# k and v of two batches laid out as nine tokens a partition, q transposed as it is loaded, and wider rows for the weights

## The chip, the cores and the metric

One Trainium2 chip, of which the kernel uses one core. Its engines run side by side, each through a list of instructions of its own: TensorE (PE, with its weight loads PEld), VectorE (DVE), ScalarE (ACT), GpSimd (POOL) and SyncE (SP), which here issues nearly all DMAs. The metric is the device time of one execution in microseconds (us), compared by the median of several runs.

## The reference

```python
kv = np.einsum('bhsd,bhse->bhde', k, v)          # q, k, v: 4 batches, 8 heads, 576 tokens, 64 wide
out = np.einsum('bhsd,bhde->bhse', q, kv)
rms = np.sqrt(np.mean(out * out, axis=-1, keepdims=True) + 1e-06)
x = out / rms * g_norm                           # then heads side by side: 2304 x 512
h = (x @ w1) * (x @ w2) @ w3                     # 512 -> 1024 -> 1024, float64 weights
x = h @ w_out                                    # 1024 -> 512
p = domain_probs / (domain_probs.sum(-1, keepdims=True) + 1e-09)
for e in range(4):
    out += p[:, e:e + 1] * (np.maximum(x @ e_w1[e], 0.0) @ e_w2[e])   # 512 -> 1024 -> 512
```

## The kernel before

The work goes through three parts. **Attention**: a `unit b p` takes two heads of batch b. It loads q, k and v of 512 of the 576 tokens as 128 partitions of four tokens each, forms k-transposed times v of both heads on PE (`outer`, L717; a fifth step takes the 64 tokens that are left, from tiles `kvr` that `rest_kv` loads for all heads of a batch), copies the two 64x64 results into a block-diagonal tile `kvb`, reorders q by token (`qs`, L733/L734), transposes it on PE (`turned`, L688), multiplies (`inner`, L745), and normalises (`normed_turned`: squares with sums on ACT, L596; a power on POOL, L609; a product on DVE, L612; a transpose; the scale by `g8`). A `rest_unit` does the 64 left tokens of two batches (L780). **The bilinear part**: products of x with w1 and w2 (`bilinear_plain`, `bilinear_pair`), their product element by element, and a product with w3 times w_out, which `row` forms beforehand. **The experts**: for each of three groups of tokens and four experts an `up` and a `down` product, in a form with seven instead of eight block products; the weights' sums and splits are made once, written to DRAM (`w2kept`, `we`) and read again for the later groups.

Large products are done as three passes of fp32r operands split in a high and a low part (`mm3`, L327 to L329; L1574 in the wide down products). The small ones of the attention are plain f32; an f32 product counts as two records on PE in the trace.

What order the instructions stand in is not written by hand. Each function adds operations with the engines that may do them, an assumed cost, and the tiles that they read and write; `Plan.order` lists them by simulated time, with priority by stage, the place in the list `FRONT` (and behind it the loops of the experts). Every engine then runs its list in that order. While PE has nothing to do at the start, two kinds of dummy products fill its list: ten of the tile `warm` (L424), and two or three (L1822) ahead of the first use of each PSUM bank that an operation of stages 1 to 3 takes:

```python
            for b in spare:
                for _ in range(FILL.get(op.prio, 0)):
                    nc.tensor.matmul(b[:, 0:P], ident, ident, start=True, stop=True)
            op.emit(e)
```

They stand in PE's list like any other, and run also when data is there. The vector g is loaded as 128 single elements on ACT's queue (L428).

Of the kernel before, what the change touches and what calls it, by code (L numbers as in the profile page):

```python
# [18 lines left out]
P = 128  # L19
RAWS = 5  # L20
# [11 lines left out]
SUMMING = 18  # L32
# [67 lines left out]
class Plan:  # L100
# [11 lines left out]
    def add(self, engines, emit, reads=(), writes=(), latency=0.2, stage=None, free=False, hold=None):  # L112
# [4 lines left out]

        op = Op(engines, emit, self.stage if stage is None else stage, latency)
# [24 lines left out]
    def order(self):  # L143
# [43 lines left out]
        while len(result) < len(ops):  # L187
# [9 lines left out]
            for e in engines:  # L197
# [26 lines left out]
                end = now + op.engines[e]  # L224
# [5 lines left out]
                op.done = end + op.latency  # L230
# [32 lines left out]
def attention_moe_kernel(  # L263
# [48 lines left out]
    plan = Plan({"r": RAWS, "h": TILES, "n": 4, "c": 2, "b": BANKS, "d": 1000, **RINGS})  # L312
# [5 lines left out]
    def bank():  # L318
        return Buf("b", "b", [P, 512], F32)

# [25 lines left out]
    def load(buf, *parts, key=None, queue="sp", cost=None):  # L346
        def emit(_):
# [6 lines left out]
            {queue: cost or (1.48 if buf.kind == "r" else 0.68)}, emit,  # L354
# [56 lines left out]
    graw = const.tile([P, 1], F32, name="graw")  # L411
# [5 lines left out]
    def constants():  # L417
        make_identity(nc, ident)
        nc.gpsimd.memset(power, -0.5)

        nc.scalar.activation(out=graw, in_=ident[:, 0:1], func=ACTF.Square)
# [27 lines left out]
    def decode(name, src, shape=None):  # L449
# [6 lines left out]
        load(raw, ((lambda t: t.rearrange("p (k f) -> p k f", k=KD)) if shape else whole, src))  # L456
# [110 lines left out]
    def rest_kv(b):  # L567
# [1287 lines left out]
```

## Time and profile before

| | before |
|---|---|
| median of 3 runs | 1107.79 us (1107.46 to 1109.48) |
| the profiled execution: its own time, its span | 1109.42 us, 1107.6 us |
| busy: PE, DVE, ACT, POOL | 99%, 78%, 56%, 4% of the span |
| chain that ended last | PE 94%, DMA 3%, ACT 1%, POOL 1% |
| DMA | 282.30 MB, mean 255 GB/s |
| granted clock of PE | 1.0 in all slices |

The span runs from the first to the last instruction. Busy time is the time in which at least one record of an engine is open; matmuls are pipelined, so that a record of PE stays open beyond the start of the next one. What one more matmul costs is therefore read from the chain or from the starts of successive rows, not from its mean duration.

### The profile page before, as it was taken

How to read it: one execution, taken by the hardware profiler on the slowest of the kernel's cores; microseconds unless marked ns; L12 is line 12 of the kernel's file. 1: busy time of each engine (PE TensorE's matmuls, PEld its weight loads, DVE VectorE, ACT ScalarE, POOL GpSimd, SP SyncE). 2: the span in 40 equal slices, each digit the busy share in tenths (PEclk: the TensorE clock that was granted, in tenths of full speed). 3: DMA queues.
4: the chain of work that ended last, by engine and by line, in shares of the span. 5: the costliest groups of instructions: out<-in, count | busy, mean ns of one | idle time of the engine just before them, and what ended most of it. 6: DMA issues, size and time to landing. Idle time of an engine off the chain costs nothing.

```text
span 1107.6 us, 18599 instructions
## 1 busy us (share of the span) xinstructions
PE 1093.7 (99%) x6376; PEld 993.9 (90%) x6376; DVE 864.2 (78%) x1723; ACT 616.5 (56%) x1500; POOL 47.0 (4%) x57
## 2 busy tenths in 40 slices
PE   7999999999999999999999999999999999999998
PEld 6888888888888999999998999999999999999998
DVE  4888888889869887878888884557788866485896
ACT  6998754656636665754564465443455555444531
POOL 4513200000000000000000000000000000000000
PEclk9999999999999999999999999999999999999999
DMA  9999993441230499988999996878779877686856
GB/s 262 292 345 331 379 359 124 135 155 37 88 103 17 156 334 352 355 304 285 353 356 355 369 348 222 284 237 283 239 240 356 298 222 257 226 290 219 278 154 196
DMA packets 176862, 282.30 MB, mean 255 GB/s; under 512 B 22144, under 2 KB 89728, under 8 KB 176768
## 3 DMA queue, kind: packets, MB, share of 16 engines
q1 hardware_dynamic: 176448, 280.85, 76.1%
q8 instruction: 50, 0.82, 0.3%
q10 hardware_dynamic: 320, 0.26, 0.1%
q14 instruction: 44, 0.36, 0.1%
HBM read 198.22 MB, written 82.84 MB: 254 GB/s over the span
## 4 chain that ended last, share of the span: by engine, by line
PE 94%; DMA 3%; ACT 1%; POOL 1%; DVE 0%; issue 0%; SPq 0%; POOLq 0%; DVEq 0%
PE b L327 24%; PE b L329 24%; PE b L328 24%; PE b L1574 18%; PE b L688 2%; DMA kv<-in_v_dram 1%; PE b L745 1%; PE b L717 1%; DMA w<-w2kept 1%; DMA graw<-in_g_norm_dram 0%; POOL ss L609 0%; DMA we<-wel 0%; DMA woraw<-in_moe_w_out_dram 0%; PE b L780 0%; ACT x L596 0%
## 5 line engine op out<-in xcount | busy, mean ns | idle before, releaser
L676 ACT COPY u<-b 128x384 f32<-128x384 f32 (+1 forms) x191 | 96.4, 505 | 209.3 <-PE b L329 202.3
L1574 PE MATMUL b<-w,hth 128*128 128x512 f32 x588 | 208.2, 394 | 0.3 <-DVE acc L1602 0.2
L1410 DVE TENSOR_TENSOR u<-u,b 128x384 f32<-128x384 f32 x144 | 79.5, 552 | 117.9 <-PE b L329 59.3
L1574 PE MATMUL b<-w,htl 128*128 128x256 f32 x588 | 153.9, 279 | 0.0
L1574 PEld LDWEIGHTS b<-w,hth 128*128 128x128 f32 x588 | 108.4, 188 | 19.0 <-DVE acc L1602 0.9
L1574 PEld LDWEIGHTS b<-w,htl 128*128 128x128 f32 x588 | 110.6, 188 | 3.8
L1602 DVE SCALAR_TENSOR_TENSOR acc<-b,pn,acc 128x512 f32<-128x512 f32 x123 | 85.5, 745 | 29.1 <-PE b L1574 28.4
L372 ACT CAST hth<-s 128x384 fp32r<-128x384 f32 x144 | 70.0, 512 | 48.3 <-DVE s L1510 45.6
L1421 ACT ACTIVATE u<-u 128x384 f32<-128x384 f32 x108 | 56.9, 527 | 44.0 <-DVE u L1410 43.7
L377 DVE TENSOR_TENSOR htl<-s,hth 128x384 fp32r<-128x384 f32 x144 | 75.4, 551 | 3.4 <-ACT hth L372 3.1
L329 PE MATMUL b<-wdh,htl 128*128 128x512 f32 x144 | 56.7, 394 | 0.0
L377 DVE TENSOR_TENSOR htl<-u,hth 128x384 fp32r<-128x384 f32 x108 | 56.0, 551 | 0.8 <-ACT hth L372 0.7
L328 PE MATMUL b<-wdl,hth 128*128 128x512 f32 x144 | 56.6, 393 | 0.0
L327 PE MATMUL b<-wdh,hth 128*128 128x512 f32 x144 | 56.0, 389 | 0.0
L372 ACT CAST hth<-u 128x384 fp32r<-128x384 f32 x107 | 51.5, 510 | 2.4 <-PE b L329 2.0
L327 PE MATMUL b<-w,hth 128*128 128x256 f32 x168 | 47.6, 284 | 1.3 <-DMA w<-w2kept 1.3
L328 PE MATMUL b<-w,hth 128*128 128x256 f32 x168 | 47.5, 283 | 0.0
L329 PE MATMUL b<-w,htl 128*128 128x256 f32 x168 | 47.5, 283 | 0.0
L327 PE MATMUL b<-th,weh 128*128 128x512 f32 x112 | 44.6, 398 | 0.2 <-ACT u L676 0.2
L329 PE MATMUL b<-th,wel 128*128 128x512 f32 x112 | 43.7, 390 | 0.0
L328 PE MATMUL b<-tl,weh 128*128 128x512 f32 x112 | 43.7, 390 | 0.0
L956 DVE TENSOR_TENSOR u<-u,b 128x512 f32<-128x512 f32 x42 | 28.7, 686 | 16.0 <-PE b L329 9.2
(297 smaller groups left out, 3165.5 us busy)
## 6 DMA issues: line engine op xcount, KB each, us to landing
w<-w2kept SPq DMA_DIRECT2D x126, 512.0 KB, 4.4
we<-we SPq DMA_DIRECT2D x240, 256.0 KB, 5.3
we<-weh SPq DMA_DIRECT2D x48, 256.0 KB, 4.4
we<-wel SPq DMA_DIRECT2D x48, 256.0 KB, 4.2
e2raw<-in_moe_w_dram SPq DMA_DIRECT2D x40, 256.0 KB, 4.5
w3raw<-in_moe_w_dram SPq DMA_DIRECT2D x16, 512.0 KB, 3.8
e1raw<-in_moe_w_dram SPq DMA_DIRECT2D x32, 256.0 KB, 4.6
w2kept<-wth SPq DMA_DIRECT2D x32, 256.0 KB, 4.4
```

The costliest lines, as they stand in the source:

```text
L327: nc.tensor.matmul(ps, w[0], x[0], start=first, stop=False, skip_group_check=more)
L328: nc.tensor.matmul(ps, w[0], x[1], start=False, stop=False, skip_group_check=more)
L329: nc.tensor.matmul(ps, w[1], x[0], start=False, stop=last, skip_group_check=more)
L372: nc.scalar.copy(to(dst.high.tile), value(src.tile))
L377: nc.vector.tensor_tensor(out=to(dst.low.tile), in0=value(src.tile), in1=to(dst.high.tile), op=ALU.subtract)
L676: lambda e: nc.scalar.copy(to(dst.tile), value(src.tile)) if e == "act"
L688: nc.tensor.transpose(ps[:, c], raw[:, c], ident)
L956: lambda _: nc.vector.tensor_tensor(out=t.tile, in0=t.tile, in1=ps.tile, op=ALU.add),
L1410: lambda _: nc.vector.tensor_tensor(out=t[:, :W], in0=base[:, :W], in1=ps[:, :W], op=ALU.add),
L1421: lambda eng: nc.scalar.activation(out=t[:, :W], in_=src[:, :W], func=ACTF.Relu)
L1574: nc.tensor.matmul(ps.tile if whole_width else ps[:, 0:256], (h.high if whole_width else h.low)[:, c], both if whole_width else raw[:, r, ...
L1602: nc.vector.scalar_tensor_tensor(out=a.tile, in0=ps.tile, scalar=sc, in1=a.tile, op0=ALU.mult, op1=ALU.add)
```

## The change

Batches 0 and 1 (`NINE`) load k and v of all 576 tokens in one piece a head: 64 partitions a head hold nine consecutive tokens each, so a row of 2,304 bytes is read where it was 1,024. Their product is `outer_by_head` (nine steps for each of two heads, each on 64 partitions and 64 columns), and `kvr` isn't needed for them. In batches 2 and 3 the left tokens come as 32 partitions of two tokens, in two tiles of four heads each, and `outer` has six steps instead of five, whose results for both heads go to PSUM partitions 0 to 63, side by side. q is transposed as it was loaded (`qs` is gone); for that each head's k-v product stands twice on the diagonal of a 128x128 block (`kvb` becomes two tiles), and the reordering by token is done by the access pattern of L612's successor (`by_token`). `rest_unit` multiplies head by head, 64 columns each. w1 and w2 are loaded as 256 rows by 256 columns (rows of 2,048 bytes instead of 1,024), the experts' first weights as 256 columns (1,024 bytes instead of 512), so the blocks f and f+1 now go together instead of f and f+4. g is loaded as a row and turned by a product on PE. `w2kept` is one DRAM buffer for each pair of operands and half, where it was one for each expert, and a read waits only for the writes of its own buffer. Some units' squares are summed on DVE instead of ACT (`EARLY`). The planner has other costs, and `FRONT` is a new list, which begins with the units of batch 1.

```diff
-SUMMING = 18
+NINE = (0, 1)
+TRAFFIC = 1.02
+MARGIN = {"act": 0.1, "dve": 0.1, "sp": 0.2}
+EARLY = (2, 3, 4, 5, 8, 15, 16)
...
 FRONT = (
-    "norm_scale, weight 0 7, unit 1 3, unit 1 2, weight 1 4, weight 1 0, unit 1 0, unit 1 1, unit 0 0, "
...
+    "norm_scale, unit 1 2, unit 1 3, weight 1 4, unit 1 1, weight 1 0, unit 1 0, unit 0 1, unit 0 2, unit "
...
-    graw = const.tile([P, 1], F32, name="graw")
+    graw = const.tile([1, P], F32, name="graw")
...
-            nc.scalar.dma_start(out=graw[i * D:(i + 1) * D], in_=g_norm.rearrange("(d o) -> d o", o=1))
-        nc.vector.tensor_scalar(out=g8, in0=graw, scalar1=float(D) ** 0.5, scalar2=None, op0=ALU.mult)
+            nc.scalar.dma_start(out=graw[:, i * D:(i + 1) * D], in_=g_norm.rearrange("(o d) -> o d", o=1))
...
-        kvr[b] = [half("kvr") for _ in (k, v)]
-        for raw, src in zip(kvr[b], (k, v)):
-            add({"pool": 0.4}, lambda _, raw=raw: nc.gpsimd.memset(raw[REM:P], 0.0), writes=[(raw, 1)])
...
+    kvr_slots = {}
+
+    def rest_kv(b, j):
+
...
+        kvr[b, j] = kvr_slots[turn, j]
+        for raw, src in zip(kvr[b, j], (k, v)):
             load(
-                raw, (lambda t: t[0:REM].rearrange("p (h d) -> p h d", d=D), rest(src, b)),
-                key=0, cost=1.05,
+                raw,
+                (
+                    lambda t: t[0:REM // 2].rearrange("p (h r d) -> p h r d", h=HP, r=2),
+                    src[b, j * HP:(j + 1) * HP, M:S, :].rearrange("h (p r) d -> p h r d", r=2),
+                ),
+                key=0, cost=0.33,
...
-        summing = SUMMING > len(summed)
+        summing = len(summed) not in EARLY
...
         def scale(e):
+            if by_token:
+                nc.vector.tensor_tensor(
+                    out=t.tile.rearrange("p (r h d) -> p h r d", r=R, h=2), in0=heads(ps.tile),
+                    in1=ss.tile.rearrange("p (h r) o -> p h r o", h=2).to_broadcast([P, 2, R, D]), op=ALU.mult,
+                )
+                return
...
     def unit(b, p):
         first = b not in kvb
         if first:
-            kvb[b] = zeroed("kvb")
+            kvb[b] = [zeroed("kvb"), zeroed("kvb")]
         loaded = []
-        for name, src in (("q", q), ("kv", k), ("kv", v)):
+        for name, src in (("q", q), ("kv", k), ("kv", v))[:1 if b in NINE else 3]:
             raw = half(name, ring="attention")
-            load(raw, (heads, head_pair(src, b, p)), cost=0.82)
+            load(raw, (heads, head_pair(src, b, p)), cost=0.8)
             loaded.append(raw)
-        qraw, ks, vs = loaded
-        if first:
-            rest_kv(b)
-        kr, vr = kvr[b]
+        qraw = loaded[0]
+        if b in NINE:
+            kv = Buf("r", "kv", [P, 2, S], F32)
+            load(kv, *(
+                (lambda t, n=n: t[:, n], src[b, 2 * p:2 * p + 2].rearrange("h (g r) d -> (h g) (r d)", g=D))
+                for n, src in enumerate((k, v))
+            ), cost=1.72)
+        else:
+            ks, vs = loaded[1:]
+            if (b, p // 2) not in kvr:
+                rest_kv(b, p // 2)
+            kr, vr = kvr[b, p // 2]
         ps = bank()
 
+        def outer_by_head(e):
+            for r in range(S // D):
+                for h in range(2):
+                    c, m = slice(h * D, (h + 1) * D), slice(r * D, (r + 1) * D)
+                    nc.tensor.matmul(
+                        ps[c, c], kv[c, 0, m], kv[c, 1, m], start=r == 0, stop=r == S // D - 1,
+                        skip_group_check=True,
+                    )
+
         def outer(e):
-            for r in range(R + 1):
+            for r in range(R + 2):
                 for h in range(2):
-                    c = slice(h * D, (h + 1) * D)
                     if r < R:
                         a, b_ = heads(ks.tile)[:, h, r, :], heads(vs.tile)[:, h, r, :]
                     else:
-                        m = slice(p * P + h * D, p * P + (h + 1) * D)
-                        a, b_ = kr[:, m], vr[:, m]
-                    nc.tensor.matmul(ps[c, c], a, b_, start=r == 0, stop=r == R)
-
-        add({"pe": 0.9}, outer, reads=[ks, vs, kr, vr], writes=[ps])
+                        at = (p % 2 * 2 + h) * 2 * D + (r - R) * D
+                        a, b_ = kr[:, at:at + D], vr[:, at:at + D]
+                    nc.tensor.matmul(
+                        ps[0:D, h * D:(h + 1) * D], a, b_, start=r == 0 and h == 0, stop=r == R + 1,
+                        skip_group_check=True,
+                    )
+
+        if b in NINE:
+            add({"pe": 1.4}, outer_by_head, reads=[kv], writes=[ps])
+        else:
+            add({"pe": 0.9}, outer, reads=[ks, vs, kr, vr], writes=[ps])
+        own, at = kvb[b][p // 2], p % 2 * 2 * P
+        parts = []
         for i in range(2):
-            c = slice(i * D, (i + 1) * D)
-            evacuate(
-                kvb[b], ps, D, lambda t, i=i, c=c: t[c, p * P + i * D:p * P + (i + 1) * D],
-                lambda t, c=c: t[c, c], key=(p, i),
-            )
-        qs = half("qs")
-
-        def by_token(t):
-            return t.rearrange("p (r h d) -> p h r d", r=R, h=2)
-
-        add(
-            {"act": t_act(512), "dve": t_fast(512)},
-            lambda e: nc.scalar.copy(by_token(qs.tile), heads(qraw.tile)) if e == "act"
-            else nc.vector.tensor_copy(out=by_token(qs.tile), in_=heads(qraw.tile)),
-            reads=[qraw], writes=[qs],
-        )
-        pq = turned(qs)
+            for h in range(2) if b in NINE else (None,):
+                d = slice(i * D, (i + 1) * D)
+                n, heads_of = (P, slice(0, 2)) if h is None else (D, slice(h, h + 1))
+                rows = slice(0, D) if h is None else slice(h * D, (h + 1) * D)
+                parts.append((own, (p, i, h)))
+                add(
+                    {"act": t_act(n, True), "dve": t_dve(n)},
+                    lambda e, d=d, heads_of=heads_of, rows=rows: (
+                        nc.scalar.copy if e == "act" else nc.vector.tensor_copy
+                    )(
+                        own[d, at:at + 2 * P].rearrange("p (h c) -> p h c", h=2)[:, heads_of, d],
+                        ps[rows, 0:P].rearrange("p (h c) -> p h c", h=2)[:, heads_of],
+                    ),
+                    reads=[ps], writes=parts[-1:], free=True,
+                )
+        pq = turned(qraw)
         qt = half("qt")
         evacuate(qt, pq, 512, whole, whole)
         po = bank()
 
         def inner(e):
-            for r in range(R):
-                c = slice(r * P, (r + 1) * P)
-                nc.tensor.matmul(po[:, c], qt[:, c], kvb[b][:, p * P:(p + 1) * P], start=True, stop=True)
-
-        add({"pe": 0.86}, inner, reads=[qt, (kvb[b], (p, 0)), (kvb[b], (p, 1))], writes=[po])
+            for j in range(4):
+                c, m = slice(j * P, (j + 1) * P), at + j // 2 * P
+                nc.tensor.matmul(po[:, c], qt[:, c], own[:, m:m + P], start=True, stop=True)
+
+        add({"pe": 0.86}, inner, reads=[qt] + parts, writes=[po])
         xr[b, p] = half("xr")
         if b == B - 1 and p < HP // 2:
-            normed_turned(po, [], xr[b, p])
+            normed_turned(po, [], xr[b, p], True)
         else:
             xt[b, p] = Pair("xt")
-            normed_turned(po, [(512, xt[b, p], whole, whole, None)], xr[b, p])
+            normed_turned(po, [(512, xt[b, p], whole, whole, None)], xr[b, p], True)
...
-            for h in range(HP):
-                c = slice(h * P, (h + 1) * P)
+            for h in range(H):
+                c = slice(h // 2 * P, (h // 2 + 1) * P)
                 for i in range(2):
-                    nc.tensor.matmul(po[:, c], qs[i][:, c], kvb[2 * g + i][:, c], start=i == 0, stop=i == 1)
-
-        add({"pe": 1.72}, inner, reads=[qs[0], qs[1], kvb[2 * g], kvb[2 * g + 1]], writes=[po])
+                    own, at = kvb[2 * g + i][h // 4], h % 4 * P + h % 2 * D
+                    nc.tensor.matmul(
+                        po[:, h * D:(h + 1) * D], qs[i][:, c], own[:, at:at + D], start=i == 0, stop=i == 1
+                    )
+
+        add({"pe": 1.72}, inner, reads=qs + kvb[2 * g] + kvb[2 * g + 1], writes=[po])
...
-            weights[n, f] = decode(f"w{n + 1}", columns((moe_w1, moe_w2)[n], f), True)
+            half_, i = divmod(f, KF // 2)
+            src = (moe_w1, moe_w2)[n][half_ * 256:(half_ + 1) * 256, i * 256:(i + 1) * 256]
+            weights[n, f] = decode(f"w{n + 1}", src.rearrange("(k p) f -> p k f", p=P), 2)
...
-        if e not in w2_kept:
-            w2_kept[e] = Buf("d", f"w2kept{e}", [P, len(W2_OPERANDS), KF // 2, 2, 256], F32, tag=f"w2kept{e}")
-        kept, n = w2_kept[e], which[1] - which[0]
+        n = which[1] - which[0]
+        for k in range(*which):
+            if (e, k, i // 2) not in w2_kept:
+                name = f"w2kept{e}_{which[0]}_{i // 2}"
+                w2_kept[e, k, i // 2] = (
+                    w2_kept[e, which[0], i // 2][0] if k > which[0]
+                    else Buf("d", name, [P, n, 2, 2, 256], F32, tag=name), k - which[0],
+                )
+        kept = w2_kept[e, which[0], i // 2][0]
         add(
             {"sp": 0.37 * n},
             lambda _: nc.sync.dma_start(
-                out=kept.tile[:, which[0]:which[1], i, part, :],
+                out=kept.tile[:, :, i % 2, part, :],
                 in_=t.tile.bitcast(F32)[:, 0:256 * n].rearrange("p (o c) -> p o c", o=n),
             ),
-            reads=[t], writes=[(kept, (which, i, part))], latency=2.4,
+            reads=[t], writes=[(kept, (i, part))], latency=2.4,
...
-        raw1, raw2 = Buf("r", "e1raw", [P, 2, 512], F32), Buf("r", "e2raw", [P, 2, 512], F32)
+        raw1, raw2 = Buf("r", "e1raw", [P, KD, 256], F32), Buf("r", "e2raw", [P, 2, 512], F32)
+        load(raw1, (whole, e_w1[e][:, i * 256:(i + 1) * 256].rearrange("(k p) f -> p k f", p=P)))
+        load(raw2, (whole, e_w2[e][i * 256:(i + 1) * 256, :].rearrange("(n p) c -> p n c", p=P)))
         fs = (i, i + KF // 2)
-        load(raw1, *(
-            (lambda t, n=n: t[:, n].rearrange("p (k f) -> p k f", k=KD), columns(e_w1[e], f))
-            for n, f in enumerate(fs)
-        ))
-        load(raw2, *((lambda t, n=n: t[:, n], e_w2[e][f * P:(f + 1) * P, :]) for n, f in enumerate(fs)))
-        w, _ = winograd_weights([raw1, raw1], [lambda t: t[:, 0], lambda t: t[:, 1]])
+        w = expert_operands(raw1)
...
     def norm_scale():
-        add({"act": 1.4}, load_norm, writes=[xscale], latency=2.5, stage=3)
+        row_ = Buf("c", "grow", None, None)
+        row_.tile = graw
+        add({"act": 1.4}, load_norm, writes=[row_], latency=3.5, stage=3)
+        ps = bank()
+        add(
+            {"pe": 0.1}, lambda _: nc.tensor.transpose(ps[:, 0:1], graw, ident[0:1, 0:1]),
+            reads=[row_], writes=[ps],
+        )
+        add(
+            {"dve": 0.2},
+            lambda _: nc.vector.tensor_scalar(
+                out=g8, in0=ps[:, 0:1], scalar1=float(D) ** 0.5, scalar2=None, op0=ALU.mult
+            ),
+            reads=[ps], writes=[xscale], free=True,
```

The experts' weight functions (`expert_operands`, `w2_sums`) form the same sums with fewer and wider DVE instructions; they add nothing to PE's list.

PE's list from its start to the first inner products, before. `warm` and the products of `ident` alone are the dummies, `kv` and `kvr` are the tiles of k and v, `qs` the reordered q:

```order
L424 MATMUL warm<-ident 128x128 x10
L1822 MATMUL b<-ident 128x128 x3
L688 MATMUL b<-ident,qs 128x128 x4
L1822 MATMUL b<-ident 128x128 x3
L717 MATMUL b<-kv 64x64 x8
L717 MATMUL b<-kvr 64x64 x2
L1822 MATMUL b<-ident 128x128 x2
L688 MATMUL b<-ident,qs 128x128 x8
L1822 MATMUL b<-ident 128x128 x3
L745 MATMUL b<-kvb,qt 128x128 x4
```

And the same stretch of the change (L756 is `outer_by_head`, L2027 the dummies, L724 the transposes, L804 `inner`):

```order
L438 MATMUL warm<-ident 128x128 x10
L2027 MATMUL b<-ident 128x128 x3
L724 MATMUL b<-ident,q 128x128 x4
L1950 MATMUL b<-ident,graw 128x1
L2027 MATMUL b<-ident 128x128 x3
L756 MATMUL b<-kv 64x64 x18
L2027 MATMUL b<-ident 128x128 x3
L724 MATMUL b<-ident,q 128x128 x4
L2027 MATMUL b<-ident 128x128 x3
L756 MATMUL b<-kv 64x64 x18
L2027 MATMUL b<-ident 128x128 x3
L804 MATMUL b<-kvb,qt 128x128 x4
```

A unit's outer product is 18 products where it was 10, and there are 24 dummies of L2027 in the whole list where L1822 had 20. In both lists all of these dummies stand ahead of the first large product. Ahead of it stand, before, 52 transposes, 8 units' outer and 7 units' inner products; in the change 56 transposes, 8 outer products of `NINE` and one of batch 3, and 8 inner products. The rows just ahead of the first large product of the change (L341; L769 is `outer` of batches 2 and 3):

```order
L804 MATMUL b<-kvb,qt 128x128 x4
L769 MATMUL b<-kv 64x64 x8
L769 MATMUL b<-kvr 64x64 x4
L724 MATMUL b<-ident,x 128x128 x4
L804 MATMUL b<-kvb,qt 128x128 x8
L724 MATMUL b<-ident,x 128x128 x4
L756 MATMUL b<-kv 64x64 x18
L724 MATMUL b<-ident,q 128x128 x4
L341 MATMUL b<-xth,wh 128x512
```

In batches 2 and 3 a unit's outer product is 12 products (rows L769) where it was 10. All other counts on PE are the same in both lists, the large products' too, except for the one transpose of g (L1950) and for `rest_unit`. There, before, PE had this row in each of the two (`qr` is the turned q of the left tokens):

```order
L780 MATMUL b<-kvb,qr 128x128 x8
```

And in the change:

```order
L840 MATMUL b<-kvb,qr 128x64 x16
```

So as many columns go through, in twice as many products. SP's list at its start, before:

```order
L349 DMA w1raw<-in_moe_w_dram 128x4x128
L349 DMA q<-in_q_dram 128x2x256
L349 DMA kv<-in_k_dram 128x2x256
L349 DMA kv<-in_v_dram 128x2x256
L349 DMA kvr<-in_k_dram 64x8x64
L349 DMA kvr<-in_v_dram 64x8x64
```

And in the change:

```order
L363 DMA q<-in_q_dram 128x2x256
L363 DMA kv<-in_k_dram 128x576
L363 DMA kv<-in_v_dram 128x576
L363 DMA q<-in_q_dram 128x2x256
L363 DMA kv<-in_k_dram 128x576
L363 DMA kv<-in_v_dram 128x576
L363 DMA w2raw<-in_moe_w_dram 128x2x256
```

The first unit's data stands first, and no transfer of `kvr` is among the first 26; the first weights come behind two units.

## Rows read from the trace of the kernel before

**Rows 1.** The page: span, busy time, and slices of 27.7 us.

```profile
span 1107.6 us, 18599 instructions
PE 1093.7 (99%) x6376; PEld 993.9 (90%) x6376; DVE 864.2 (78%) x1723; ACT 616.5 (56%) x1500; POOL 47.0 (4%) x57
...
PE   7999999999999999999999999999999999999998
...
PEclk9999999999999999999999999999999999999999
```

**Rows 2.** Windows: start:end and length, busy time (records) of each engine, clock, DMA.

```profile
core 0: us, PE busy (x) PEld busy (x) DVE busy (x) ACT busy (x) POOL busy (x), PEclk, DMA share, GB/s
0.00:10.00 10.00, 7.10 (x52) 6.80 (x52) 1.61 (x4) 3.80 (x6) 6.71 (x19) 1.00 0.88 213
...
30.00:40.00 10.00, 9.48 (x111) 8.15 (x111) 8.23 (x16) 9.94 (x60) 6.64 (x7) 1.00 1.13 270
40.00:60.00 20.00, 20.00 (x129) 17.02 (x129) 16.91 (x32) 18.58 (x76) 9.19 (x9) 1.00 1.08 313
...
1080.00:1107.60 27.60, 23.10 (x193) 22.89 (x191) 18.00 (x40) 3.88 (x8) 0.00 (x0) 1.00 0.63 196
```

**Rows 3.** The chain that ended last, around 50 and 103 us: start, length, what.

```profile
50.51 0.73 PE b L717 x20
51.24 0.59 PE b L688 x4
...
53.22 0.44 PE b L688 x4
...
55.05 0.89 PE b L745 x8
...
103.70 1.79 PE b L780 x16
```

**Rows 4.** PE's timeline: start, length, records, idle time before and its end.

```profile
1.34 4.64 PE L424 MATMUL warm<-ident 128*128 128x128 f32 x20 [1.34 <-POOL ident masks.py:199]
5.77 0.88 PE L1822 MATMUL b<-ident 128*128 128x128 f32 x6
...
19.86 0.69 PE L717 MATMUL b<-kv 128*64 128x64 f32 x16 [1.70 <-DMA kv<-in_v_dram]
...
36.71 0.48 PE L327 MATMUL b<-xth,wh 128*128 128x512 f32 x1
...
50.44 0.69 PE L717 MATMUL b<-kv 128*64 128x64 f32 x16
50.95 0.29 PE L717 MATMUL b<-kvr 128*64 128x64 f32 x4
51.17 0.66 PE L688 MATMUL b<-ident,qs 128*128 128x128 f32 x4
```

**Rows 5.** Weight loads and products of L717 and L780: durations in ns.

```profile
L717 PEld LDWEIGHTS b<-kv x256: 132/138/138, 9.0 to 111.3; 128*64 128x64 f32 x128
L717 PE MATMUL b<-kv x256: 222/222/271, 9.0 to 111.4; 128*64 128x64 f32 x128
...
L780 PEld LDWEIGHTS b<-kvb,qr x32: 190/192/192, 103.4 to 127.4; 128*128 128x128 f32 x32
L780 PE MATMUL b<-kvb,qr x32: 275/275/275, 103.5 to 127.5; 128*128 128x128 f32 x32
```

**Rows 6.** DMA in the first 45 us: GB/s in 40 slices, totals, issues.

```profile
GB/s 0 44 293 362 309 272 168 173 312 251 260 266 343 369 355 351 342 351 291 168 167 223 283 288 277 301 322 357 350 317 180 181 217 212 295 348 350 348 278 176
DMA packets 15446, 12.09 MB, mean 269 GB/s; under 512 B 4637, under 2 KB 15442, under 8 KB 15442
...
kvr<-in_k_dram SPq DMA_DIRECT2D x4, 128.0 KB, 8.2
```

**Rows 7.** ACT's groups ahead of the first large product: count, busy, mean ns.

```profile
L596 ACT ACTIVATE x<-b 128x64 f32<-128x64 f32 x49 | 10.2, 249 | 1.2 <-PE b L745 1.2
...
L733 ACT COPY qs<-q 128x512 f32<-128x512 f32 x5 | 3.1, 614 | 0.0
```

**Rows 8.** PE's timeline at the one long stop behind the front.

```profile
486.65 0.39 PE L327 MATMUL b<-w,hth 128*128 128x256 f32 x1 [1.32 <-DMA w<-w2kept]
```

More of the change, by code (lines that the diff above doesn't have):

```diff
@@ L110, in __init__, with add @@
         self.stage = 0
-    def add(self, engines, emit, reads=(), writes=(), latency=0.2, stage=None, free=False, hold=None):
+    def add(self, engines, emit, reads=(), writes=(), latency=None, stage=None, free=False, hold=None):
+        if latency is None:
+            latency = 0.2 if "pe" in engines else 0.04
         op = Op(engines, emit, self.stage if stage is None else stage, latency)
@@ L223, in order @@
                     queue[o].remove(op)
-                end = now + op.engines[e]
+                end = now + op.engines[e] * (TRAFFIC if e == "sp" else 1.0)
                 if e in op.ported:
@@ L229, in order @@
                 free_at[e] = end
-                op.done = end + op.latency
+                op.done = end + op.latency + MARGIN.get(e, 0.0)
                 result.append((op, e))
@@ L455, in decode @@
         raw = Buf("r", name + "raw", [P, 512], I64)
-        load(raw, ((lambda t: t.rearrange("p (k f) -> p k f", k=KD)) if shape else whole, src))
+        load(raw, ((lambda t: t.rearrange("p (k f) -> p k f", k=shape)) if shape else whole, src))
         val, add_ = half("val", ring="decoded"), half("add", I32, "decoded")
@@ L618, in normed_turned @@
         if summing:
-            add({"act": 8 * t_act(D, True)}, square, reads=[ps], writes=[t, ss])
+            add({"act": 1.75}, square, reads=[ps], writes=[t, ss])
         else:
@@ L622, in normed_turned @@
             add({"dve": t_dve(512)}, total, reads=[t], writes=[ss], free=True)
-        add({"pool": 1.91}, root, writes=[ss], hold=0.3)
+        add({"pool": 2.2}, root, writes=[ss], hold=0.3)
         add({"dve": t_dve(512)}, scale, reads=[ps, ss], writes=[t], free=True)
@@ L669, in zeroed @@
         t = half(name)
-        add({"pool": 0.5}, lambda _: nc.gpsimd.memset(t.tile, 0.0), writes=[t])
+        cleared(t, (0, P))
         return t
@@ L759, in rest_unit @@
             (lambda t: t[0:REM].rearrange("p (h d) -> p h d", d=D), rest(q, 2 * g)),
-            (lambda t: t[REM:P].rearrange("p (h d) -> p h d", d=D), rest(q, 2 * g + 1)), cost=1.5,
+            (lambda t: t[REM:P].rearrange("p (h d) -> p h d", d=D), rest(q, 2 * g + 1)), cost=2.0,
         )
@@ L998, in bilinear_pair @@
         if g:
-            for j, f in enumerate((f0, f1)):
-                multiplied(B, f, [w[j] for w in ws])
+            for f in (f0, f1):
+                multiplied(B, f, ws)
             return
@@ L1330, in w2_sums @@
             raw = Buf("r", "e2raw", [P, 2, 512], F32)
-            load(raw, *(
-                (lambda t, n=n: t[:, n], e_w2[e][f * P:(f + 1) * P, :]) for n, f in enumerate((i, i + KF // 2))
-            ))
-        def part(n, c):
-            return lambda: [raw[:, n, c * 256:(c + 1) * 256]]
-        def own(t, c):
-            return lambda: [t[:, c * 256:(c + 1) * 256]]
-        t12, t34 = half("t12"), half("t34")
-        lo, hi = slice(0, 256), slice(256, 512)
-        combined("t1", 256, part(0, 1), part(0, 0), ALU.subtract, [raw], t12, lo)
@@ L1344, in w2_sums @@
-        combined("t2", 256, part(1, 1), own(t12, 0), ALU.subtract, [raw, (t12, 0)], t12, hi)
-        combined("t3", 256, part(1, 1), part(0, 1), ALU.subtract, [raw], t34, lo)
-        combined("-t4", 256, part(1, 0), own(t12, 1), ALU.subtract, [raw, (t12, 256)], t34, hi)
-        for t, which in ((t12, (3, 5)), (t34, (5, 7))):
-            s = Pair("wt")
-            split(s, t, 512)
+            load(raw, (whole, e_w2[e][i * 256:(i + 1) * 256, :].rearrange("(n p) c -> p n c", p=P)))
+        t23 = half("t23")
@@ new lines, in sums @@
+        def sums(make, reads, writes, n):
+            add({"dve": t_dve(n)}, make, reads=reads, writes=writes)
+        sums(
+            lambda _: nc.vector.tensor_tensor(
+                out=raw[:, 0, 0:256], in0=raw[:, 0, 256:512], in1=raw[:, 0, 0:256], op=ALU.subtract
+            ), [], [raw], 256,
+        )
+        sums(
+            lambda _: nc.vector.tensor_tensor(
+                out=t23[:, :].rearrange("p (o c) -> p o c", o=2),
+                in0=raw[:, 1, 256:512].unsqueeze(1).to_broadcast([P, 2, 256]),
+                in1=raw[:, 0].rearrange("p (o c) -> p o c", o=2), op=ALU.subtract,
+            ), [raw], [t23], 512,
+        )
@@ new lines, in w2_sums, with two @@
+        sums(
+            lambda _: nc.vector.tensor_tensor(
+                out=raw[:, 1, 0:256], in0=raw[:, 1, 0:256], in1=t23[:, 0:256], op=ALU.subtract
+            ), [t23], [raw], 256,
+        )
+        t14 = Pair("wt")
+        def two(t):
+            return t.rearrange("p (o c) -> p o c", o=2)
+        add(
+            {"act": t_act(512), "dve": t_fast(512)},
+            lambda eng: nc.scalar.copy(two(t14.high.tile), raw[:, :, 0:256]) if eng == "act"
+            else nc.vector.tensor_copy(out=two(t14.high.tile), in_=raw[:, :, 0:256]),
+            reads=[raw], writes=[t14.high],
+        )
@@ L1350, in w2_sums @@
+        add(
+            {"dve": t_dve(512)},
+            lambda _: nc.vector.tensor_tensor(
+                out=two(t14.low.tile), in0=raw[:, :, 0:256], in1=two(t14.high.tile), op=ALU.subtract
+            ),
+            reads=[raw, t14.high], writes=[t14.low],
+        )
+        t23s = Pair("wt")
+        split(t23s, t23, 512)
+        for s, which in ((t14, (5, 7)), (t23s, (3, 5))):
             for n, p in enumerate(s.parts):
@@ L1456, in up @@
         c21 = copied(acc)
-        times(third, "s3", "t3")
+        times(third, "-s3", "-t3")
         times(acc, "s1", "t1", True)
```

172 lines of the change are left out of this document (138 added, 34 removed), and 22 rows, old and new, of the table FRONT.

## The prediction

> **What bounds the kernel now.** I read the page first: PE is busy for 1093.7 of 1107.6 us and its clock is granted in full [rows 1]. Busy time of pipelined records says little about slack, so the windows come next: PE is busy without a break from 40 us on, waits in the first 40, and has 4.5 us of the last 27.6 in which only the end of the output is left [rows 2]. ACT is as full as PE between 30 and 40 us (9.94 of 10), but nothing behind 40 us waits for it long enough to show on PE. The chain is PE for 94% of the span, and its pieces give what a record costs without overlap [rows 3]. So the kernel is PE's list: a record added to it lengthens the span by its price, unless it falls into a wait, and a wait can be won back in two places alone, the front and the stop of 1.32 us for a read of `w2kept` at 486.65 us [rows 8]. The rest of the stops behind 40 us are a few tenths each.
>
> **The front now.** The first dummy starts at 1.34 us, the first large product at 36.71 [rows 4]: 35.4 us. In between lie 20 `warm` records, 4.4 us to the next row; 40 records of the other dummies, 52 transposes and 56 records of inner products, all of 128 columns, at 0.111 (8 in 0.89 [rows 3]): 16.4; and 8 outer products at 0.73 and the 0.15 by which the transposes behind them are longer (0.59 against 0.44 [rows 3]): 7.0. That is 27.8 us of records and **7.6 of waits**, most of them for k and v (1.70 at 19.86 us [rows 4]). The transfers explain it: where the 256-byte rows of `kvr` run, the rate falls from some 350 to some 170 GB/s [rows 6].
>
> **The change on PE, record by record.** A record of 64 columns on half of the array: 16 take 0.51 us (50.44 to 50.95, with the entry), and by columns it is a quarter of 0.111 if two run side by side; so 28 to 32 ns, and I take 30. A half alone then gives one in 60 (bounds 30, if records don't run side by side at all, and 64).
> Outer products of batches 0 and 1: 36 records instead of 20, on the two diagonal quarters in turn. No row shows quarters. If they run side by side as the halves do, 16 x 30 ns = +0.48 a unit, **+3.8** for eight; if not, 36 x 60 instead of 20 x 30, +1.56 a unit, +12.5. I take the first, since the two halves also shared a bank of PSUM and each quarter has rows, columns and partitions of its own.
> The Trainium skill speaks against this (TensorEngine Tiling, Gotcha 1: PSUM Pressure): tiles on different rows of the array can't access the same PSUM bank at the same time, and here both quarters write to one bank, though to different partitions of it. By that rule the sum below would be 8.6 us higher; no run here shows it.
> Outer products of batches 2 and 3: both heads now write to partitions 0 to 63, so both sit on the same half and nothing runs beside them. 24 records x 60 = 1.44 instead of 0.60: +0.84 a unit, **+6.7** for eight (bounds +0.12 x 8 = 1.0 and +7.5).
> `rest_unit`: 32 records of 64 columns instead of 16 of 128 at 1.79 us. A weight load of 128 columns lasts 192 ns and one of 64 columns 138 [rows 5]; 54 ns for 64 columns makes 108 for 128, as long as the 0.112 of a whole record here [rows 3]. So the weights alone keep the pace, and half the columns are no cheaper: +1.79 twice, **+3.6** (bounds 0, if columns set the pace, and 3.6).
> Dummies: 4 products, 8 records, **+0.9**. The turn of g, a record of another form: **+0.2**. In sum +15.2.
>
> **What it takes away.** In the front, PE's work ahead of the first large product becomes 4.4 + (48 + 56 + 64) records x 0.111 = 18.6 + 8 x (0.88 + 0.48) = 10.9 + 1.72 for the one unit of batch 3 + 0.2 = 35.8 us, from 1.34 on: not before 37.1 us even if it never waits. And it will hardly wait: the 9 units and 2 weights that stand ahead there are some 8.8 MB, all in rows of 1,024 bytes and more but for one small `kvr`; at the 350 GB/s that such stretches show [rows 6] they take 25 us, and are in by 28. k and v of a unit now hold one of five raw buffers until PE is done with them, which can hold SP up, but only as long as PE itself is behind. ACT loses the copies of q (5 x 0.61 [rows 7]) and the sums of squares of five early units, and gains two small copies a unit; it is no longer the fullest engine. I leave 0.6 us of waits (bounds 0 and 7.6): **-7.0**.
> The stop at 486.65 us: PE waits for a read that now depends only on its own two weights' writes, not on those of the whole expert. I take **-1.3** (bounds 0 and -1.5). What comes late next is the read's own 4.4 us behind the writes, which nothing shortens; the order around it is a new one.
> At nothing I cost: wider rows of w1 and w2 and of the experts' weights, since PE didn't wait for those transfers; the DVE and ACT work that goes away behind 40 us, since PE is busy throughout there, which is the cover (if PE did wait there, the gain would be a few tenths); g's load, on which only `g8` waits. The tail is as before.
>
> **Sum.** 15.2 - 7.0 - 1.3 = +6.9 us. The profiled execution took 1109.42 us with a span of 1107.6; the median of the runs is 1107.79, so the profiled one is 1.6 above it. I add the sum to the median: **1114.7 us**.
>
> **Rivals.**
> (1) The quarters don't run side by side: 8 x 36 x 30 ns = +8.6 on top, 1123.3 us. For it speaks the shared bank; against it that the two quarters have no row, column or partition in common. 0.14. (The Trainium skill's rule on banks, TensorEngine Tiling, Gotcha 1, would have it so.)
> (2) Columns, not weights, set the pace in `rest_unit`: -3.6, 1111.1 us. The loads of rows 5 speak against it; that a load could be hidden behind the product before it speaks for it. 0.10.
> (3) The other side: 30 ns is what 64 columns cost one after another, in any place of the array, and the two halves never overlapped. Then batches 2 and 3 pay +1.0 instead of +6.7, and `rest_unit` 64 records x 30 = 1.9 instead of 3.6, -1.7 instead of +3.6: 1103.7 us, faster. It decides from about 46 ns a record downward. Against it: 128 columns cost 111, nearly four times 30, and a product's length grows by 53 ns from 64 to 128 columns (222 to 275 [rows 5]), so 64 columns alone take some 53. 0.07.
> (4) The front wins nothing: the waits for data become waits for ACT's and POOL's chain of normalising, or for raw buffers, and the first large product comes at 43 us: +5 to +7, 1120 to 1121.5 us. Windows speak for it (ACT at 9.94 of 10), the list against it, with PE's own 35.8 us. 0.08.
> That the change doesn't do what it says is true of one part: PE is free earlier of data, but not of work.
>
> **How the numbers follow.** Forecast (1112 to 1117.5) 0.58, the rivals 0.14, 0.10, 0.07, 0.08, and 0.03 for what I don't see. The range of 1107.5 to 1121.5 leaves out rivals 1 and 3, some 0.2. A measurement here tells 0.2% from nothing, 2.2 us. Faster than 1105.6: rival 3, 0.07. Within 0.2%: parts of rivals 2 and 3 and better luck in the front, 0.10. Slower: 0.83.
>
> **What the profile after would show.** PE's first large product at 37 to 39 us with hardly a wait ahead of it; pieces of `outer_by_head` of 36 records in about 1.1 us (2.1 by rival 1); of `outer` of 24 records in 1.4 to 1.5 (0.75 by rival 3); of `rest_unit` of 32 records in 3.6 (1.8 by rival 2); no stop for `w2kept` near 490 us; behind 40 us PE busy throughout. The prediction is wrong if a half alone takes records at 30 ns, or if the new order opens stops behind the front, which I can't read from a list.

## The result, and the profile after

The changed kernel takes 1115.28 us (median of 4 runs, 1113.61 to 1116.56); the kernel before, beside it on the same chip, 1108.55 (4 runs, 1107.46 to 1109.48). The ratio is 1.006 with an interval of 1.0042 to 1.0078: the change makes it slower by 0.6%. The forecast was 1114.7 us. The profiled execution took 1114.81 us, with a span of 1113.0; the one of before had 1107.6 [rows 1].

The page of after, as in [rows 1]:

```profile
span 1113.0 us, 18828 instructions
...
PE 1106.1 (99%) x6577; PEld 1008.8 (91%) x6577; DVE 864.4 (78%) x1692; ACT 607.3 (55%) x1401; POOL 50.9 (5%) x69
...
PE   9999999999999999999999999999999999999998
```

PE has 201 records more than before, which is the list's own count: 128 for batches 0 and 1, 32 for batches 2 and 3, 32 for `rest_unit`, 8 dummies and the turn of g. The first slice now stands at 9 tenths or more; it was at 7.

Windows of the front, with the columns of [rows 2]:

```profile
0.00:10.00 10.00, 8.66 (x81) 8.29 (x82) 0.16 (x1) 2.75 (x7) 8.65 (x23) 1.00 0.80 250
10.00:20.00 10.00, 9.45 (x133) 8.83 (x132) 5.41 (x12) 7.25 (x44) 3.71 (x4) 1.00 1.06 382
...
30.00:40.00 10.00, 10.00 (x121) 9.21 (x118) 8.26 (x17) 8.55 (x49) 7.94 (x11) 1.00 1.09 327
```

PE, which waited all through the front before, is busy from its first record on but for one gap, and ACT has fallen from 9.94 to 8.55 of 10 between 30 and 40 us. PE's timeline names that gap, the first large product (the row of L341), and the stop that answers to [rows 8]:

```profile
1.34 4.51 PE L438 MATMUL warm<-ident 128*128 128x128 f32 x20 [1.34 <-POOL ident masks.py:199]
...
18.42 1.16 PE L804 MATMUL b<-kvb,qt 128*128 128x128 f32 x8 [0.55 <-ACT kvb L788]
...
37.97 0.47 PE L341 MATMUL b<-xth,wh 128*128 128x512 f32 x1
...
498.97 0.36 PE L341 MATMUL b<-w,hth 128*128 128x256 f32 x1 [0.38 <-DMA w<-w2kept]
```

No transfer of q, k or v is waited for any more, and yet the first large product comes 1.26 us later than at 36.71 [rows 4]: PE now waits for nothing there, because it has more to do. What a record costs is read from the chain that ended last, as in [rows 3]:

```profile
20.69 1.20 PE b L756 x36
21.88 0.59 PE b L724 x4
...
32.08 1.54 PE b L769 x24
...
88.06 3.52 PE b L840 x32
```

These are the outer product of batches 0 and 1 (L756), the transposes behind it, the outer product of batches 2 and 3 (L769) and the rest unit (L840). Durations of single records, in ns (least, median, most):

```profile
L756 PE MATMUL b<-kv x288: 218/218/267, 7.9 to 37.4; 64*64 64x64 f32 x144
...
L769 PE MATMUL b<-kv x128: 222/222/271, 32.0 to 106.6; 128*64 128x64 f32 x128
...
L840 PEld LDWEIGHTS b<-kvb,qr x64: 188/192/192, 87.8 to 114.7; 128*128 128x128 f32 x64
L840 PE MATMUL b<-kvb,qr x64: 217/275/275, 87.9 to 114.7; 128*128 128x64 f32 x64
```

L756 and L769 last equally long (218 and 222 ns), although one is passed through PE at twice the rate of the other. A pipelined record's duration does not tell its price; the step from one start to the next does. For L756 these steps alternate between some 7 and some 52 ns: the records start in pairs, one pair every 58 ns, which makes 29 ns a record. For L769 the median step is 58 ns, without pairs, and for L840 112 ns.

Summing all steps by shape, from the records of the two traces, shows where the time went (a wait counts with the record before it):

```
us (records)                        before           after
128x128, full array            55.97 (428)     48.83 (404)   warm, dummies, transposes, inner products, waits of the front
64 columns on one half         13.43 (320)     12.20 (192)
64 columns on quarters             -            9.56 (288)
64 columns on the full array       -            6.98 (64)
turn of g                          -            0.15 (1)
large products               1032.08 (5627)  1029.28 (5627)
sum                          1101.47         1107.00
```

The small shapes with the waits of the front cost 8.3 us more (77.72 against 69.40). The large products, whose count is unchanged, cost 2.8 less. That is hardly one execution's chance: the change once more (below) has 1029.07 us for them, its variants 1028.4 to 1030.9, and the two variants of before 1031.8 and 1032.8.

### The profile page after: what moved, and what is told of

Read it like the earlier page. It is cut to its first block, busy times and chain, and to the rows that moved or that the text cites. A ratio compares the mean times of both kernels' runs of the same rounds, so it can differ in the third digit from the quotient of the medians.

```text
span 1113.0 us, 18828 instructions
## 1 busy us (share of the span) xinstructions
PE 1106.1 (99%) x6577; PEld 1008.8 (91%) x6577; DVE 864.4 (78%) x1692; ACT 607.3 (55%) x1401; POOL 50.9 (5%) x69
## 4 chain that ended last, share of the span: by engine, by line
PE 99%; DVE 0%; ACT 0%; issue 0%; POOL 0%; POOLq 0%
PE b L343 25%; PE b L341 25%; PE b L342 25%; PE b L1763 18%; PE b L724 2%; PE b L804 1%; PE b L769 1%; PE b L756 1%; PE b L840 1%; PE b L2027 1%; PE warm L438 0%; ACT x L626 0%; DVE acc L1881 0%; DVE htl L391 0%; DVE acc L1791 0%
## 5 line engine op out<-in xcount | busy, mean ns | idle before, releaser
L341 PE MATMUL b<-wdh,hth 128*128 128x512 f32 x144 | 56.0, 389 | 0.0
L341 PE MATMUL b<-w,hth 128*128 128x256 f32 x168 | 47.8, 285 | 0.5 <-DMA w<-w2kept 0.4
L341 PE MATMUL b<-th,weh 128*128 128x512 f32 x112 | 43.8, 391 | 0.0
```

The costliest lines, as they stand in the source:

```text
L341: nc.tensor.matmul(ps, w[0], x[0], start=first, stop=False, skip_group_check=more)
```

## The experiments

All ratios are to the kernel before, run on the same chip in the same set. Three theories stand against each other: that of the prediction (PE's list sets the time, a half alone takes a record in 60 ns, weights set the pace of `rest_unit`), its rivals 2 and 3 (columns set the pace; 30 ns is the price anywhere), and one on the front (whatever PE is spared there comes back as waits for data).

**The change once more** (no edit), to have it beside the experiments of its set.

> The change itself once more, as a measure for the others of this set: 1115.3 us, 1.006 of the kernel before.

Measured: 1115.85 us (5 runs), before 1108.33, ratio 1.0068 (1.0053 to 1.0084), span 1112.7. It stays within the interval of the first set.

**Batches 2 and 3 on two halves.** Head 0 goes to PSUM partitions 0 to 63 again and head 1 to 64 to 127; four small copies take the place of two.

```diff
-                    nc.tensor.matmul(
-                        ps[0:D, h * D:(h + 1) * D], a, b_, start=r == 0 and h == 0, stop=r == R + 1,
-                        skip_group_check=True,
-                    )
+                    c = slice(h * D, (h + 1) * D)
+                    nc.tensor.matmul(ps[c, c], a, b_, start=r == 0, stop=r == R + 1, skip_group_check=True)
...
-            for h in range(2) if b in NINE else (None,):
+            for h in range(2):
```

> The change with one part altered: in batches 2 and 3 the outer products of the two heads go to PSUM partitions 0 to 63 and 64 to 127 again (two halves of the array in turn), with four small copies a unit instead of two. My theory (a half alone takes a record in 58 ns, two halves in turn in 29): a unit's 24 records fall from 1.54 to 0.85 us, 8 x 0.69 = 5.6 us less than the change, 1109.7 us. If records cost the same wherever they stand: no difference, 1115.3. If the extra copies on ACT become the limit: between the two.

Measured: 1109.46 us (11 runs), before 1109.26 (28 runs), ratio 1.0000 (0.9991 to 1.0009), span 1107.4. That is 5.6 us less span than the change. Its chain, the outer product now on L770:

```profile
32.73 0.85 PE b L770 x24
...
83.50 3.52 PE b L838 x32
...
100.74 1.55 PE b L770 x48
```

The same 24 records take 0.85 us instead of 1.54, on the same data and in the same order. So a half alone does pay double, and what the change gave up was a neighbour. Rival 3, which put a half alone at the same 30 ns, falls. The rest unit (here L838) stays at 3.52, as it should.

**`rest_unit` with two heads a product.** 128 columns once instead of 64 twice; the two heads' columns are picked from the doubled block by an access pattern.

```diff
-            for h in range(H):
-                c = slice(h // 2 * P, (h // 2 + 1) * P)
+            for h in range(HP):
+                c = slice(h * P, (h + 1) * P)
                 for i in range(2):
-                    own, at = kvb[2 * g + i][h // 4], h % 4 * P + h % 2 * D
-                    nc.tensor.matmul(
-                        po[:, h * D:(h + 1) * D], qs[i][:, c], own[:, at:at + D], start=i == 0, stop=i == 1
-                    )
+                    own = kvb[2 * g + i][h // 2].tile.rearrange("p (j k d) -> p j k d", j=2, d=D)
+                    nc.tensor.matmul(po[:, c], qs[i][:, c], own[:, h % 2, 0:4:3], start=i == 0, stop=i == 1)
```

> The change with one part altered: the product of the left tokens joins two heads again, 16 records of 128 columns in each of the two units instead of 32 of 64. Theory (the weight load sets the pace): 3.52 us a unit become 1.79, 2 x 1.73 = 3.5 us less, 1111.8. If this stretch isn't on the path: no difference, 1115.3.

Measured: 1112.12 us (8 runs), ratio 1.0031 (1.0021 to 1.0041), span 1110.2, 2.8 less than the change. In its chain:

```profile
80.34 1.54 PE b L769 x24
...
88.48 1.79 PE b L840 x16
```

Half as many records over the same number of columns take half the time, 112 ns each either way. So it is the record, not its 64 or 128 columns of data, that is paid for, and rival 2 falls. In every one of these records 128 columns of weights are loaded; a record of L769, with the same 64 columns of data but only 64 of weights, goes through in 58 ns. The Trainium skill has the time of a weight load go by its columns (TensorE: Matmul & The Clock Gate, LDWEIGHTS); by its formula 128 columns are an estimate of 107 ns. The measured step of 112 ns is close to that.

**The change without the dummies of L2027, and before without those of L1822.** In both kernels:

```diff
-FILL = {1: 3, 2: 3, 3: 2}
+FILL = {}
```

> The change without the 24 dummy products of L2027 (the ten of warm stay). Theory (the front of the change is bound by PE's own list): the 48 records of 0.111 us fall out of it, 5.3 us less, of which some tenths come back as waits; 4 to 5.3 us less, 1110 to 1111.3. If the front waits for data or for ACT all the same: no difference, 1115.3. If the clock falls without the dummies: more than 1115.3, and the granted clock shows it.

> The kernel before without its 20 dummy products of L1822. Theory (its front is bound by waits, and the dummies lie in them): no difference, 1108.5 within 1 us. If dummies cost their time in any front: 40 x 0.111 = 4.4 us less, 1104.

Measured in the change: 1112.08 us (9 runs), ratio 1.0027 (1.0018 to 1.0037), span 1109.6. In before: 1108.52 (11 runs), ratio 0.9991 (0.9982 to 1.0), no difference. The change's timeline without them:

```profile
11.44 0.66 PE L724 MATMUL b<-ident,q 128*128 128x128 f32 x4 [0.28 <-DMA q<-in_q_dram]
15.57 0.63 PE L724 MATMUL b<-ident,q 128*128 128x128 f32 x4 [1.13 <-DMA q<-in_q_dram]
...
34.15 0.47 PE L341 MATMUL b<-xth,wh 128*128 128x512 f32 x1
```

Of 48 records less (5.3 us) 1.4 come back as two waits for q, and the first large product comes 3.8 us earlier. In before the same edit moves that product nowhere, from 36.71 to 36.79; its timeline shows the waits that grew, and its windows something more:

```profile
6.12 0.66 PE L688 MATMUL b<-ident,qs 128*128 128x128 f32 x4 [0.79 <-ACT qs L733]
8.38 1.12 PE L717 MATMUL b<-kv 128*64 128x64 f32 x16 [1.60 <-DMA kv<-in_v_dram]
...
12.59 1.12 PE L688 MATMUL b<-ident,qs 128*128 128x128 f32 x4 [2.21 <-ACT qs L733]
...
36.79 0.48 PE L327 MATMUL b<-xth,wh 128*128 128x512 f32 x1
```

```profile
10.00:12.00 2.00, 0.38 (x4) 0.19 (x4) 1.64 (x3) 0.60 (x2) 0.00 (x0) 0.50 1.10 350
...
18.00:20.00 2.00, 2.00 (x11) 2.00 (x11) 1.30 (x2) 1.65 (x7) 1.36 (x1) 0.50 1.09 348
20.00:22.00 2.00, 2.00 (x26) 1.57 (x25) 1.80 (x5) 1.96 (x16) 0.45 (x2) 0.61 1.29 247
```

The column behind POOL's is the granted clock: behind a gap of 0.79 us and within the one of 1.60 it falls to 0.50 (1.2 GHz), where it still stands from 18 to 20 us; with the dummies it was 1.00. Even that costs before nothing: the first large product stays where it was, so its front goes by its waits, for q, k and v and for what ACT makes of them, and PE has slack at either clock. The dummies lie in waits there; in the change there are hardly any waits left for them to lie in, and they stand on the path.

**All three edits together**: two halves, two heads a product, no dummies.

> The change with the three alterations together: heads on two halves again, left tokens in pairs of heads, no L2027 dummies. Theory (PE's list bounds the whole, so single gains add up): 5.8 + 3.2 + 3.2 = 12.2 us less than the change, 1103 us, ratio 0.995 to the kernel before. If the same wait is won three times over (the gains overlap): 1106 to 1109.

Measured: 1103.40 us (6 runs), before 1108.33, ratio 0.9955 (0.994 to 0.9971), span 1101.4. It is 12.4 below the change of its set and 4.9 below before: faster than both. The three edits apart came to 5.6 + 2.8 + 3.4 = 11.8 us of span; together 11.6 of 1113.0. So the gains add, as they should if all three are only records on one list. Its timeline:

```profile
8.42 1.26 PE L756 MATMUL b<-kv 64*64 64x64 f32 x36 [0.22 <-DMA kv<-in_v_dram]
11.33 0.66 PE L724 MATMUL b<-ident,q 128*128 128x128 f32 x4 [0.55 <-DMA q<-in_q_dram]
15.52 0.63 PE L724 MATMUL b<-ident,q 128*128 128x128 f32 x4 [1.27 <-DMA q<-in_q_dram]
...
33.41 0.48 PE L341 MATMUL b<-xth,wh 128*128 128x512 f32 x1
```

**No batch as nine tokens**, in the change and in the kernel with the three edits:

```diff
-NINE = (0, 1)
+NINE = ()
```

> The change with no batch in NINE: k and v of batches 0 and 1 as four tokens a partition and the left ones apart, like batches 2 and 3 of the change. Theory (the front is bound by PE): a unit's outer product becomes 24 records on one half, 1.54 us, instead of 36 on two quarters, 1.20: 8 x 0.34 = 2.7 us more, 1118.0. If the nine tokens are what ended the waits of the front: up to 7 us of waits come back, 1120 to 1125.

> The three alterations and no batch in NINE: a unit's outer product is 24 records on two halves, 0.85 us, where the three alterations alone have 1.20 in batches 0 and 1. If PE bounds the front: 8 x 0.35 = 2.8 us less than with the three alone, 1100. If without dummies the front is bound by data again, then the left tokens' small rows cost waits: as much as the three alone or up to 3 us more, 1103 to 1106.

Measured in the change: 1116.52 us (5 runs), ratio 1.0075 (1.0059 to 1.0091); 0.7 above the change of its set by medians, 3.0 by spans (1115.7 and 1112.7). The sign is that of the theory on PE's list; between 0.7 and 3.0 the size stays open, since the two intervals overlap. Its front has no wait of 0.2 us or more for q, k or v either, though the left tokens of all batches are loaded apart again, and its first large product comes at 41.66 us. So the up to 7 us of waits that the other theory expected back stay away: as long as PE's list is this long, with the dummies and the products on a half alone, it isn't the nine tokens that keep the waits out. In the kernel with the three edits: 1104.35 (6 runs), ratio 0.9966 (0.9953 to 0.9978), span 1102.9. Here four tokens on two halves have eight units x (36 - 24) x 29 ns = 2.8 us less on PE, and the time is not lower. The timeline and the windows say why:

```profile
12.57 0.66 PE L724 MATMUL b<-ident,q 128*128 128x128 f32 x4 [1.91 <-DMA q<-in_q_dram]
...
25.47 0.69 PE L770 MATMUL b<-kv 128*64 128x64 f32 x16 [1.09 <-DMA kv<-in_v_dram]
...
35.34 0.48 PE L341 MATMUL b<-xth,wh 128*128 128x512 f32 x1
```

```profile
12.00:14.00 2.00, 1.43 (x12) 1.43 (x12) 0.95 (x2) 1.54 (x4) 1.77 (x5) 0.92 1.13 278
14.00:16.00 2.00, 1.69 (x26) 1.42 (x25) 1.05 (x3) 1.55 (x16) 2.00 (x3) 0.50 1.06 319
16.00:18.00 2.00, 1.79 (x15) 1.36 (x12) 1.82 (x4) 1.67 (x8) 1.83 (x3) 0.73 1.10 349
```

The waits for q, k and v are back, the clock goes to 0.50 between 14 and 16 us, behind the gap of 1.91, and the first large product comes 1.9 us later than with nine tokens, although one inner product (8 records) fewer stands ahead of it. So with the shorter list the nine tokens win at least as much in the front as their records cost on PE. The two medians, 1103.40 and 1104.35, have intervals that overlap.

**`w2kept` as one buffer for each expert again** in the change, and the other way round **before with one for each pair of operands and half**. The edit in the change (in before it is the reverse):

```diff
-                    else Buf("d", name, [P, n, 2, 2, 256], F32, tag=name), k - which[0],
...
+            w2_kept[e] = Buf("d", f"w2kept{e}", [P, len(W2_OPERANDS), KF // 2, 2, 256], F32, tag=f"w2kept{e}")
```

> The change with w2kept as one DRAM buffer for each expert again, so that a read waits for all writes of that expert. My theory in the prediction (the read near 490 us waits for writes that it doesn't need): the stop for w2kept is back at some 1.5 us where the change has 0.8 in two pieces, +0.6 us, 1116. If the stop comes from where the reads stand in the queue, not from the buffers: 0.8 us or less of it as before, 1115.3 to 1115.9.

> The kernel before with w2kept as one DRAM buffer for each pair of operands and half, the one edit of the change on this stop; its order around the experts shifts a little, since the planner sees other waits. Prediction's step (the wait for the whole expert's writes makes the stop): the stop of 1.32 us near 487 us is gone or under 0.3, time 1107.2, 1.3 below the kernel before. Rival (the read of the pair just written is itself late, whichever buffer it lies in, so that the stop depends on the order and varies from one execution to the next): a stop for w2kept of 0.3 to 1.4 us may stand there still, and the time is 1108.5, within 0.1% of before.

Measured: the change with the old buffers takes 1114.41 us (6 runs), ratio 1.0048 (1.0033 to 1.0064); its trace has no stop of 0.2 us or more for `w2kept`. Before with the new buffers takes 1108.48 (12 runs), ratio 1.0008 (0.9996 to 1.002), and still stops:

```profile
484.08 0.39 PE L327 MATMUL b<-w,hth 128*128 128x256 f32 x1 [0.73 <-DMA w<-w2kept]
```

The change once more, the same kernel as the one that stopped for 0.38 us:

```profile
494.77 0.39 PE L341 MATMUL b<-w,hth 128*128 128x256 f32 x1 [0.81 <-DMA w<-w2kept]
```

The stop is there with either kind of buffer and at another place from one execution to the next: 0.81 us in one piece here, 0.38 us there, with a second piece of 0.30 us (by the steps of its records) at 501.50. In the other variants with the new buffers it ranges from none of 0.2 us or more to 1.1 us (the kernel with all three edits). The theory that the buffers set it falls. That the read is late by itself fits, but both edits also shift the order around the experts, and no run isolates the cause, which stays open.

**g as 128 single elements again**, so no turn on PE.

```diff
-            nc.scalar.dma_start(out=graw[:, i * D:(i + 1) * D], in_=g_norm.rearrange("(o d) -> o d", o=1))
+            nc.scalar.dma_start(out=graw[i * D:(i + 1) * D], in_=g_norm.rearrange("(d o) -> d o", o=1))
```

> The change with g loaded as 128 single elements again, without the turn on PE. Theory (only the scale waits for it, and the front is bound by PE): -0.2 us for the product that PE is spared, no difference that can be measured, 1115.3. If the small elements hold up the first k and v: up to 2 us more, 1117.

Measured: 1116.08 us (6 runs), ratio 1.0062 (1.0047 to 1.0077). It can't be told from the change.

## Why the prediction was right, point by point

- **PE's list sets the time.** Held: three edits that only change PE's records moved the span by what their records cost, alone and together.
- **Outer products of batches 0 and 1, +3.8.** Measured 1.20 - 0.73 = 0.47 a unit, 3.8 for eight. The quarters do run side by side: a pair of records every 58 ns, 29 ns a record, half of what a half alone pays. Rival 1 wanted about 2.1 us for the 36 records and falls; so does, for this pair of tiles, the reading of the Trainium skill's rule (TensorEngine Tiling, Gotcha 1: PSUM Pressure) by which tiles on different rows have to take turns at one bank. Here they share the bank and not its partitions, and the trace shows no turns.
- **Outer products of batches 2 and 3, +6.7.** Measured 1.54 - 0.73 = 0.81, 6.5 for eight; taken back by the experiment with two halves, 5.6 us of span.
- **`rest_unit`, +3.6.** Measured 3.52 - 1.79 = 1.73, twice: 3.5; taken back by two heads a product, 2.8 us of span.
- **Dummies +0.9, turn of g +0.2.** 8 records and 0.15 us. What the prediction didn't say is that all 48 records of these dummies, not only the 8 added ones, had moved from waits onto the path: without them the change wins 3.4 us of span, before nothing.
- **The front, -7.0.** The first large product was to come at 37 to 39 us with 0.6 us of waits ahead: it came at 37.97, with one wait of 0.55. Rival 4 falls. With the records above, +15.2 - 7.0 = +8.2 was forecast for the small shapes and the front; the sums by shape give +8.3, and less the records as measured (3.8 + 6.5 + 3.5 + 0.9 + 0.15) that leaves some -6.5 for the front. The reason given, that the transfers are in by 28 us in their wider rows, is only in part shown: without the nine tokens the waits stay away as well, as long as PE's list is as long.
- **The stop for `w2kept`, -1.3.** This term failed, in size and in reason. The stop didn't go: it was 0.38 us with its second piece in one execution and 0.81 in another. Reckoned like the sums by shape, from start to start beyond a usual step, it is 1.48 us in the one profile of before against 0.54 + 0.30 and 0.97, so the term is worth some -0.5 to -0.6 in these executions, and not by way of the buffers, as the two experiments on them show.
- **Against rival 3.** Rival 3 fell by the experiment with two halves, not by the prediction's argument that a record's duration grows by 53 ns from 64 to 128 columns (222 to 275 [rows 5]). The records of L840 have 64 columns of data and a median of 275 ns too, so that growth isn't the price of the columns of data.
- **What offset it.** The large products together cost 2.8 us less and not 1.3. By the starts of their records two other stops of before, 0.41 us at 203.5 and 0.32 at 731.5, are not there in after, and the rest is spread over the list in tenths. This comes with the new order; no run takes it apart.

The sum, +6.9 on a median of 1107.79, thus met 1115.28 partly by luck: between the two profiled executions the difference is 5.4 us (1114.81 - 1109.42), close to the 5.5 of the sums by shape (8.3 - 2.8), and between the medians of the two sets with the change 6.7 and 7.5. Executions of before alone lie as far apart as that, 1106.42 to 1112.79 in the largest set.

## What to carry to other kernels

On an engine whose list sets the time, price a product by the steps from one start to the next, averaged over it and its neighbours: a 64-column product on half of the array is cheap only while its neighbour uses the other half, and a narrower product with as wide a weight load saves nothing. When waits for data are taken out of a stretch, look again at everything that was free because it lay in them, dummy products first. And a stop that moves between executions of one kernel is no ground for a term of a sum until a second execution shows it.

## What the runs showed of the hardware that was not expected

- Two diagonal quarters of the array (64 rows by 64 columns each), in turn, take f32 records at 29 ns each, in pairs 58 ns apart, as two halves do, though both write to one PSUM bank, on different partitions.
- A stretch of 64-column records on quarters or halves between records of the full array has a fixed cost: the four transposes behind them take 0.59 us where others take 0.44 [rows 3], and 24 records on halves take 0.85 while 48 in a row take 1.55, that is 24 x 29 ns and some 0.15 us once.
- In the kernel before without its dummies PE's granted clock stood at 0.50 for over 10 us of the front, and the time was the same: the lower clock costs nothing where PE waits for data anyway. In the kernel with three edits and four tokens a gap of 1.91 us stood ahead of a stretch at 0.50; gaps of 0.55 and 1.27 us in the kernel with three edits left the clock at 1.00.
